# Forming the values of an attention step two visits later, with four transposed-probability tiles

## The chip, the cores and the metric

The kernel runs on one core of one Trainium2 chip. The metric is the device time of one execution in microseconds (us). Before the change it was 578.66 us, the median of 3 runs (578.45 to 579.55). One more execution was recorded by the hardware profiler; all times of single instructions below are from that one.

## What is computed

Attention over 4 batches, 8 heads, 768 positions and head size 64, with a mask that keeps the first 8 positions and the 96 nearest earlier ones, and a bias that falls with the distance. The result, reshaped to 3072 tokens of 512 channels, goes through a gated feed-forward:

```python
scores = scale * (q @ k.T) + bias            # masked: is_global | is_local
a = softmax(scores);  x = (a @ v) as (3072, 512)
h = ((x @ w1) * (x @ w2)) @ w3
out = h @ w_out
```

The kernel multiplies w3 by w_out once at the start (`fold`), so the feed-forward of a block of tokens is three products: x with w1, x with w2, and their product g with w3·w_out. Each factor is held as a rounded high part and a low part (`split`), and each product takes three matmuls: high by high, high by low, low by high.

## The kernel before, in words

The 12 blocks of 256 query positions (4 batches, 3 blocks each) times 4 pairs of heads make 48 units; two units make a *step*, so there are n = 24 steps, two to a block and four to a pair of blocks (512 tokens). A *visit* is what the program does around one step. Its parts, in the order in which TensorE (PE) gets them:

- `visit` (L541): the scores of step s for its first unit (`scores`, tile `s`), one half of the *values* of step s-1 (`values`, tile `v`: probabilities times v), the scores of the second unit, the other half of the values. Between the halves ScalarE (ACT) writes a few elements of the values' tile (L553), so all that stands behind it on ACT waits for the first half.
- `rows` (L412): VectorE (DVE) adds the bias and finds the row maximum (L424), ACT takes exp (L425). `take` (L531) splits the values of step s-1 into the feed-forward's input `xh`, `xl`, and when a block is complete puts its feed-forward on the list `work`.
- `slices(k)` (L512): k *slices* from that list. A slice is half of a product group: 12 matmuls of 256 columns or 6 of 512, or 6 of the output product. They fill PE while DVE, ACT and the DMA engines bring the probabilities of step s into shape.
- `loads` (L519): SyncE's queue (SP) loads the keys and queries (`qr`) and the v rows (`vr`) of step s+1.
- `softmax` (L428) scales the rows. From step SWAP = 4 on they are then transposed without PE: DVE transposes blocks of 32 by 32 (`swap`, L468) into a tile `ph`, one DMA per unit writes it to a buffer `d` in DRAM (L469), and four DMAs per unit read it back with the blocks exchanged (`back`, L474), into the same `ph`. Only then are the probabilities of step s ready for `values` in visit s+1.

The first four steps (`first_steps`, L579) run beside the preparation of the weights (`weights`, `convert`, `fold`) and transpose on PE (`flip`). The order on PE, and on ACT from visit 4 on, is the order in which the program is written; on DVE and SP it is so in the first steps, and later a scheduler places DVE's and SP's instructions. An engine and a queue run what they hold in order: a DMA on SP that waits holds up all DMAs behind it.

Buffers: `ph` has 2 tiles (those of one step), `vr` 4 (two steps), `qr` 2, `a` and `g` of the feed-forward 2 each. The table `SLICES` says how many slices each visit has: 10 in visit 3, 9 in visits 4 to 7, 12 from visit 8 on. The first two blocks give 24 slices each and every later pair of blocks 48, so 12 per visit use up what four visits bring; what the last pair leaves is run at the end.

Of the kernel before, what the change touches and what calls it, by code (L numbers as in the profile page):

```python
# [10 lines left out]
F32 = mybir.dt.float32  # L11
# [9 lines left out]
P = 128  # L21
NP = H // 2
NQ = 2
# [46 lines left out]
class FeedForward:  # L70
# [29 lines left out]
    def weights(self, *names):  # L100


        pieces, fresh = [], []
        for kind, *at in names:
            if kind == "w":
                f, n = divmod(at[0], 2)

                raw = self.stage[{3: 0, 5: 2, 6: 0}[f] + n] if f in (3, 5, 6) else self.raws[:, n]
                dst, src = self.t3s[:, at[0] % 4], self.src[n][f]
                fresh.append((n, f, dst.bitcast(F32).rearrange("p (i m) -> p i m", i=NCC)))  # L110
            elif kind == "o":
                dst, src = self.wo[:, at[0]], self.w_out[at[0]]
            else:
                f, z = at
                dst = self.mp.tile([P, PC], I32, tag=self.next(0, "agagoo"), name=f"t3_{f}_{z}")
                src = self.w3t[f, :, z * PC:(z + 1) * PC]
                self.t3[f, z] = dst
            if kind != "w":
                raw = self.next(1, self.stage + self.first)
            pieces.append((dst, raw, src))  # L120
        convert(self.nc, pieces)
        self.lows()
        for n, f, x in fresh:
            hi, lo = (w[:, f] for w in self.w[n])
            self.nc.scalar.activation(hi, x, AF.Copy)
            self.late.append((lo, x, hi))
        if names[0] == ("o", NFC - 2):

            self.first = []
# [22 lines left out]
    def run(self, c, xh, xl, row, width):  # L152
# [4 lines left out]
        for f0 in range(0, NFC, nf):  # L157
            fs = slice(f0, f0 + nf)
            for n in range(2):
# [9 lines left out]
                if n == 0:  # L169
                    a = mp.tile([P, nf, width], F32, tag="a", name=f"a_{c}_{f0}")  # L170
                    nc.scalar.activation(a, ps, AF.Copy)  # L171
                    yield
            g = mp.tile([P, nf, width], F32, tag="g", name=f"g_{c}_{f0}")
            nc.vector.tensor_tensor(out=g, in0=ps, in1=a, op=ALU.mult)  # L174
            split(nc, gh[:, fs], gl[:, fs], g)
            yield
# [151 lines left out]
def banded(ctx, tc, ff, ns, nt, nf, oki, ident, qk, vx):  # L328
# [6 lines left out]
    ld = ctx.enter_context(tc.tile_pool(name="ld", bufs=STEP))  # L335
    at = ctx.enter_context(tc.tile_pool(name="at", bufs=2))
    ps_s = ctx.enter_context(tc.tile_pool(name="ps_s", bufs=1, space=PSUM))
    ps_v = ctx.enter_context(tc.tile_pool(name="ps_v", bufs=1, space=PSUM))
# [9 lines left out]
    def biases():  # L348
        it = at.tile([P, UW], I32, tag="ph", name="it")
        itg = at.tile([P, P], I32, tag="ph", name="itg")  # L350
        rel, loc = (at.tile([P, UW], F32, tag="pr", name=n) for n in ("rel", "loc"))
# [38 lines left out]
    def load_values(c, hp):  # L390
        b, cb = divmod(c, NCB)
        nw = 2 * NQ if cb else 2 * NQ - 1
        vr = ld.tile([P, 2 * NQ, 2 * D], F32, tag="vr", bufs=2 * STEP, name=f"vr_{c}_{hp}")
        nc.sync.dma_start(out=vr[:, :nw], in_=vx[b, cb, hp, :, :nw])
        return vr
# [59 lines left out]

    def swap(c, hp, pr):

        first = c % NCB == 0  # L460
        x = at.tile([P, 2, NB, NQ * 2, BK], F32, tag="ph", name=f"ph_{c}_{hp}")
        d = dr.tile([NB, BK, 2, NB, NQ * 2 * BK], F32, tag="d", name=f"d_{c}_{hp}")
# [77 lines left out]

    def visit(s, ahead):  # L541


        uu = spread(s - 1) if s else None
        ps = [None, None]
# [4 lines left out]
        def half(k):  # L550
            if s:
                if k:
                    nc.scalar.activation(uu[:, :, T], ident[:, :STEP], AF.Copy)  # L553
                values(uu, s - 1, k)

# [7 lines left out]
        return ps, uu  # L563

    def first_visit(s):
        ps, uu = visit(s, False)
        if s:
            take(s - 1, uu)
        return ps
# [4 lines left out]
    def turn(s, i, prs):  # L574
        c, hp = pairs(s)[i]
        phs.setdefault(s, []).append(at.tile([P, NQ * 2, 2, P], F32, tag="ph", name=f"ph_{c}_{hp}"))
        flip(c, hp, prs[i][0], phs[s][i])

    def first_steps():  # L579
# [27 lines left out]
        ff.weights(("o", 6), ("o", 7))  # L607
        loads(0, keys=False)
        prs = all_rows(0, ps)
# [9 lines left out]
        def scale(s):  # L619
            for p, r in zip(pairs(s), prs):  # L620
                softmax(*p, *r, nc.scalar)
            loads(s + 1)

# [53 lines left out]

    SLICES = [()] * 3 + [(5, 3, 2)] + [9] * 4 + [12] * (n - 8)
    with tc.manual_schedule(engines={mybir.EngineType.PE}):
        with tc.manual_schedule(engines={mybir.EngineType.DVE, mybir.EngineType.SP}):  # L680
            first_steps()
        with tc.manual_schedule(engines={mybir.EngineType.Activation}):
            for s in range(4, n):
                ps, uu = visit(s, True)
                rs = []
                for i, p in enumerate(pairs(s)):
                    rs.append(rows(*p, ps[i]))
                    if i == 0:
                        take(s - 1, uu)
                slices(2)  # L690
                loads(s + 1)
                xd = []
                for p, r in zip(pairs(s), rs):
                    softmax(*p, *r, nc.vector)
                    xd.append(swap(*p, r[0]))
                for x, d in xd:
                    back(x, d)
                phs[s] = [x for x, _ in xd]
                slices(SLICES[s] - 2)
            uu = spread(n - 1)  # L700
            values(uu, n - 1, 2)
            take(n - 1, uu)
            slices(10 ** 6)
# [45 lines left out]
```

## Time and profile before

| | before |
|---|---|
| median of 3 runs | 578.66 us |
| the profiled execution: device time | 575.89 us |
| its span (first to last instruction) | 574.0 us |
| PE busy | 537.0 us (94%) |
| DVE busy | 308.8 us (54%) |
| ACT busy | 243.1 us (42%) |
| moved by DMA | 96.06 MB, mean 167 GB/s |
| PE waiting for `ph<-d` before a values matmul | 13.3 us in 9 waits |

PE is the engine that is nearly always at work; matmuls are pipelined, so its busy share says that it is seldom without work, not that each matmul runs at peak. The program has three stretches: to about 107 us the weights are prepared (DVE is busy 47 to 48 of every 50 us), from 107 to 499 us steps 4 to 23 are visited, and from 499 us to the end there is only feed-forward. The granted clock of TensorE is given as a share of full speed: 1.00 is the upper of its two levels (2.4 GHz), 0.50 the lower (1.2 GHz).

### The profile page before, as it was taken

Reading aid. Unit: us, or ns where it says so; the run is one execution under the profiler, and the core shown is the slowest. Engines: PE = TensorE matmul, PEld = TensorE weight load, DVE = VectorE, ACT = ScalarE, POOL = GpSimd, SP = SyncE. Lnnn points to the kernel's source line nnn. Section 1 sums busy time; section 2 is a strip of 40 time slices with the busy share of each in tenths; the row PEclk is TensorE's granted clock in tenths of the full one; section 3 lists DMA queues with packets and bytes.
Section 4 is the critical chain, followed back from the end, with each engine's and each line's share of the span. In section 5 each row is a group of like instructions: output and inputs, shape, how many; then the busy total and the mean of one; then the engine's idle time right before and its main releaser. Section 6 shows DMA issues by size and latency. Waiting matters only on the chain.

```text
span 574.0 us, 11298 instructions
## 1 busy us (share of the span) xinstructions
PE 537.0 (94%) x4280; PEld 429.1 (75%) x4280; DVE 308.8 (54%) x931; ACT 243.1 (42%) x716; POOL 5.0 (1%) x22
## 2 busy tenths in 40 slices
PE   1999998979888999999999999999999998999995
PEld 0445547968887888888888888888888886888884
DVE  8999999644543574554447624754365565012200
ACT  3065687525442554345435424553355344122210
POOL 0000000000000000000000000000000000000000
PEclk9999999998989999999999999999999999999998
DMA  8897654254466646456554576455665542500011
GB/s 299 302 362 273 226 222 155 84 165 173 142 198 201 199 139 187 158 191 197 174 165 168 163 222 207 139 139 173 212 221 156 169 152 81 176 19 1 1 38 42
DMA packets 72527, 96.06 MB, mean 167 GB/s; under 512 B 5904, under 2 KB 48912, under 8 KB 72464
## 3 DMA queue, kind: packets, MB, share of 16 engines
q1 hardware_dynamic: 72464, 95.25, 50.8%
q8 instruction: 36, 0.59, 0.5%
q14 instruction: 27, 0.22, 0.1%
HBM read 67.96 MB, written 27.26 MB: 166 GB/s over the span
## 4 chain that ended last, share of the span: by engine, by line
PE 58%; DMA 12%; ACT 10%; DVE 9%; SPq 8%; issue 2%; DVEq 0%; ACTq 0%
PE m L164 8%; PE m L165 8%; PE m L166 8%; SPq L474 7%; PE o L181 7%; PE o L182 6%; PE o L183 6%; DMA ph<-d 6%; ACT pr L425 6%; PE w L145 5%; PE v L502 5%; DMA d<-ph 4%; PE s L409 3%; ACT pr L437 1%; DMA stage<-w3t 1%
## 5 line engine op out<-in xcount | busy, mean ns | idle before, releaser
L425 ACT ACTIVATE pr<-pr,mx 128x232 f32<-128x232 f32 (+1 forms) x192 | 88.1, 461 | 23.3 <-DVE mx L424 23.3
L424 DVE CUSTOM_DVE_ANT_0 pr<-s,biasw 128x232 f32<-128x232 f32 x160 | 54.3, 395 | 55.6 <-PE s L409 55.4
L164 PE MATMUL m<-xh,w2h 128*128 128x512 f32 (+1 forms) x224 | 81.6, 364 | 1.4 <-DVE g L174 1.4
L174 DVE TENSOR_TENSOR g<-m,a 128x512 f32<-128x512 f32 x48 | 32.9, 685 | 92.4 <-PE m L166 92.4
L164 PE MATMUL m<-xh,w1h 128*128 128x512 f32 (+1 forms) x224 | 81.2, 363 | 0.3 <-ACT a L171 0.3
L165 PE MATMUL m<-xl,w1h 128*128 128x512 f32 (+1 forms) x224 | 80.6, 360 | 0.0
L166 PE MATMUL m<-xh,w1l 128*128 128x512 f32 (+1 forms) x224 | 80.5, 360 | 0.0
L166 PE MATMUL m<-xh,w2l 128*128 128x512 f32 (+1 forms) x224 | 80.4, 359 | 0.0
L165 PE MATMUL m<-xl,w2h 128*128 128x512 f32 (+1 forms) x224 | 80.4, 359 | 0.0
L66 ACT ACTIVATE gh<-g 128x512 fp32r<-128x512 f32 x48 | 30.3, 632 | 114.0 <-DVE g L174 114.0
L181 PE MATMUL o<-wh,gh 128*128 128x512 f32 x192 | 76.2, 397 | 0.0
L182 PE MATMUL o<-wl,gh 128*128 128x512 f32 x192 | 75.1, 391 | 0.0
L183 PE MATMUL o<-wh,gl 128*128 128x512 f32 x192 | 74.9, 390 | 0.0
L145 PE MATMUL w<-wo,t 128*128 128x512 f32 x128 | 59.5, 619 | 11.7 <-DVE wo L61 11.3
L502 PE MATMUL v<-ph,vr 64*64 64x64 f32 (+4 forms) x1408 | 48.9, 253 | 16.6 <-DMA ph<-d 13.3
L502 PEld LDWEIGHTS v<-ph,vr 64*64 64x64 f32 (+3 forms) x1408 | 44.2, 138 | 21.2 <-DMA ph<-d 7.4
L145 PEld LDWEIGHTS w<-wo,t 128*128 128x128 f32 x128 | 24.5, 197 | 41.5 <-issue 24.9
L67 DVE TENSOR_TENSOR gl<-g,gh 128x512 fp32r<-128x512 f32 x48 | 33.2, 693 | 29.4 <-ACT gh L66 29.4
L468 DVE STREAM_TRANSPOSE ph<-pr 128x512 f32<-128x512 f32 x80 | 46.6, 640 | 3.9 <-ACT pr L437 2.8
L164 PEld LDWEIGHTS m<-xh,w2h 128*128 128x128 f32 x224 | 42.3, 189 | 8.2 <-DVE g L174 1.6
L164 PEld LDWEIGHTS m<-xh,w1h 128*128 128x128 f32 x224 | 42.6, 190 | 7.1 <-ACT a L171 0.5
L171 ACT ACTIVATE a<-m 128x512 f32<-128x512 f32 x48 | 28.4, 592 | 45.0 <-PE m L166 45.0
(86 smaller groups left out, 682.1 us busy)
## 6 DMA issues: line engine op xcount, KB each, us to landing
d<-ph SPq DMA_DIRECT2D x40, 512.0 KB, 2.7
ph<-d SPq DMA_DIRECT2D x160, 128.0 KB, 3.2
qr<-qk SPq DMA_DIRECT2D x32, 312.0 KB, 3.1
vr<-vx SPq DMA_DIRECT2D x32, 256.0 KB, 4.2
stage<-w3t SPq DMA_DIRECT2D x15, 512.0 KB, 6.3
out_dram<-ot SPq DMA_DIRECT2D x24, 256.0 KB, 2.8
raws<-w SPq DMA_DIRECT2D x10, 512.0 KB, 5.7
qr<-qk SPq DMA_DIRECT2D x16, 260.0 KB, 3.3
```

The costliest lines, as they stand in the source:

```text
L145: nc.tensor.matmul(ps, lhsT=self.t3[f, z][:, i * P:(i + 1) * P].bitcast(F32), rhs=self.wo[:, k].bitcast(F32), start=k == 0, stop=k == NFC - 1)
L164: nc.tensor.matmul(ps[:, z], lhsT=mh, rhs=xh[:, i], start=i == 0, stop=False)
L165: nc.tensor.matmul(ps[:, z], lhsT=mh, rhs=xl[:, i], start=False, stop=False)
L166: nc.tensor.matmul(ps[:, z], lhsT=ml, rhs=xh[:, i], start=False, stop=i == NCC - 1)
L181: nc.tensor.matmul(ps, lhsT=gh[:, f, ts], rhs=self.wh[:, f], start=f == 0, stop=False)
L182: nc.tensor.matmul(ps, lhsT=gh[:, f, ts], rhs=self.wl[:, f], start=False, stop=False)
L183: nc.tensor.matmul(ps, lhsT=gl[:, f, ts], rhs=self.wh[:, f], start=False, stop=f == NFC - 1)
L424: nc.vector.tensor_tensor_reduce(out=pr[:, j, u, w0:], in0=ps[u][:, j, w0:UW], in1=bias, scale=-SCALE, scalar=3.0e38, op0=ALU.add, op1=ALU ...
L425: nc.scalar.activation(pr[:, j, u, w0:], pr[:, j, u, w0:], AF.Exp, bias=m, scale=-1.0, accum_out=sm[:, j, u:u + 1])
L468: nc.vector.transpose(x[:, k, :, u0:], units[:, u0:, k0:k0 + P].rearrange("p u (b c) -> p b u c", c=BK))
L474: nc.sync.dma_start(out=x[b * BK:(b + 1) * BK].rearrange("r k a u c -> r k a (u c)"), in_=d[:, :, :, b].rearrange("a r k e -> r k a e"))
L502: nc.tensor.matmul(uu[u * D:(u + 1) * D, i, j * P + q:j * P + q + n], lhsT=v[r], rhs=x[:, q // step:(q + n) // step][r], start=k != 1 and ...
```

## The change

The values of step s are formed in visit s+2 instead of s+1. Steps 0 to 3 keep their old place (the values of step 3 are formed in visit 4); visit 5 therefore forms no values, visit 6 those of step 4, and so on; after visit 23 come the values of step 22, 12 slices, and the values of step 23 (`last_visit`).

So two steps' probabilities live at once: `ph` gets two tags, `ph0` and `ph1`, of two tiles each. The v rows of step s are loaded one visit later than before (with visit s+1), and `vr` has 2 tiles instead of 4. The two `g` tiles go: the product is written over `a`. Two of the early w3 tiles, which used the place of `g`, use that of `ph1`. As a block is complete one visit later, visits 4 to 8 have 7, 7, 7, 7 and 8 slices (36 in all, before 9, 9, 9, 9 in visits 4 to 7) and 12 from visit 9 on.

```diff
-            g = mp.tile([P, nf, width], F32, tag="g", name=f"g_{c}_{f0}")
-            nc.vector.tensor_tensor(out=g, in0=ps, in1=a, op=ALU.mult)
-            split(nc, gh[:, fs], gl[:, fs], g)
+            nc.vector.tensor_tensor(out=a, in0=ps, in1=a, op=ALU.mult)
+            split(nc, gh[:, fs], gl[:, fs], a)
...
-        vr = ld.tile([P, 2 * NQ, 2 * D], F32, tag="vr", bufs=2 * STEP, name=f"vr_{c}_{hp}")
+        vr = ld.tile([P, 2 * NQ, 2 * D], F32, tag="vr", name=f"vr_{c}_{hp}")
...
-    def visit(s, ahead):
+    def visit(s, sv, ahead):
-        uu = spread(s - 1) if s else None
+        uu = None if sv is None else spread(sv)
...
-            if s:
+            if uu is not None:
...
-                values(uu, s - 1, k)
+                values(uu, sv, k)
...
+    def last_visit(s):
+        uu = spread(s)
+        values(uu, s, 2)
+        take(s, uu)
...
-        loads(0, keys=False)
         prs = all_rows(0, ps)
...
-            loads(s + 1)
+            loads(s + 1, vals=False)
+            loads(s, keys=False)
...
-    SLICES = [()] * 3 + [(5, 3, 2)] + [9] * 4 + [12] * (n - 8)
+    SLICES = [()] * 3 + [(5, 3, 2)] + [7, 7, 7, 7, 8] + [12] * (n - 9)
...
-            for s in range(4, n):
-                ps, uu = visit(s, True)
+            for s in range(SWAP, n):
+                sv = s - 1 if s == SWAP else s - 2 if s > SWAP + 1 else None
+                ps, uu = visit(s, sv, True)
...
-                loads(s + 1)
+                loads(s + 1, vals=False)
+                if s > SWAP:
+                    loads(s - 1, keys=False)
...
-                    xd.append(swap(*p, r[0]))
+                    xd.append(swap(*p, r[0], f"ph{s % 2}"))
...
-            uu = spread(n - 1)
-            values(uu, n - 1, 2)
-            take(n - 1, uu)
+            last_visit(n - 2)
+            loads(n - 1, keys=False)
+            slices(SLICES[n - 1])
+            last_visit(n - 1)
             slices(10 ** 6)
```

What this makes of the order on PE is seen in visit 6. The rows stand as the program has them: line, operation, output<-inputs with their numbers, and the columns. Before, behind the scores of the first unit (`s`), come the values of step 5 (`ph_2`, `ph_3` with `vr_2`, `vr_3`):

```order
L409 MATMUL s_101<-qr_0_1340 64x168
L409 MATMUL s_102<-qr_0_1340 64x168
L502 MATMUL v_2_1457<-ph_2_1354,vr_2_1139 64x128 x2
L502 MATMUL v_2_1457<-ph_3_1365,vr_3_1141 64x128 x2
L502 MATMUL v_2_1457<-ph_2_1354,vr_2_1139 64x64 x2
L502 MATMUL v_2_1457<-ph_3_1365,vr_3_1141 64x64 x2
```

After the change, in the same place, they are the values of step 4 (`ph_0_1138` and `ph_1_1149`, written in visit 4):

```order
L410 MATMUL s_101<-qr_0_1274 64x168
L410 MATMUL s_102<-qr_0_1274 64x168
L503 MATMUL v_0_1351<-ph_0_1138,vr_0_1278 64x128 x2
L503 MATMUL v_0_1351<-ph_1_1149,vr_1_1280 64x128 x2
L503 MATMUL v_0_1351<-ph_0_1138,vr_0_1278 64x64 x2
L503 MATMUL v_0_1351<-ph_1_1149,vr_1_1280 64x64 x2
```

Nothing else of the attention moves on PE: scores and values alternate as before, with values one step older.

On SP's queue, the DMAs of step 6 before: out to `d` (L469), back into `ph` (L474), then keys (`qr`) and v rows (`vr`) of step 8, then `d` of step 7:

```order
L469 DMA d_0_1573<-ph_0_1572 128x1024
L469 DMA d_1_1585<-ph_1_1584 128x1024
L474 DMA ph_0_1572<-d_0_1573 32x8x128 x4
L474 DMA ph_1_1584<-d_1_1585 32x8x128 x4
L387 DMA qr_0_1791<-qk 128x624
L387 DMA qr_1_1793<-qk 128x624
L394 DMA vr_0_1795<-vx 128x512
L394 DMA vr_1_1797<-vx 128x512
L469 DMA d_2_1806<-ph_2_1805 128x1024
L469 DMA d_3_1818<-ph_3_1817 128x1024
```

After the change (L470, L475, L388, L395 are the same operations), where the scheduler has placed the first key load of step 8 ahead of the way back of step 6, and the v rows are those of step 6:

```order
L470 DMA d_0_1469<-ph_0_1468 128x1024
L470 DMA d_1_1481<-ph_1_1480 128x1024
L388 DMA qr_0_1664<-qk 128x624
L475 DMA ph_0_1468<-d_0_1469 32x8x128 x4
L475 DMA ph_1_1480<-d_1_1481 32x8x128 x4
L388 DMA qr_1_1666<-qk 128x624
L395 DMA vr_0_1668<-vx 128x384
L395 DMA vr_1_1670<-vx 128x384
L470 DMA d_2_1679<-ph_2_1678 128x1024
L470 DMA d_3_1691<-ph_3_1690 128x1024
```

The key load takes the place of the tile that the first scores of visit 7 read, so the way back of step 6 now stands behind those scores. The v rows of step 6 follow it, and are wanted in visit 8.

## Rows read from the trace of the kernel before

**Rows 1.** The page's head: the span and its instructions, and the busy time of each engine with its share and its instructions.

```profile
span 574.0 us, 11298 instructions
PE 537.0 (94%) x4280; PEld 429.1 (75%) x4280; DVE 308.8 (54%) x931; ACT 243.1 (42%) x716; POOL 5.0 (1%) x22
```

**Rows 2.** Whom PE waited for in the whole program: us in total, number of waits, the longest.

```profile
PE v L502 <- DMA ph<-d: 13.3, 9, 3.6
PE w L145 <- DVE wo L61: 11.3, 1, 11.3
...
PE m L164 <- DVE g L174: 1.4, 1, 1.4
```

**Rows 3.** Busy time by stretches that begin with the first scores of a visit: visits 4 to 8 (9, 9, 9, 9 and 12 slices), and visits 11 and 12. Columns: the stretch in us from the span's start, its length, busy us of PE, weight loads, DVE, ACT and GpSimd with their instructions, the granted clock, the DMA engines' share, GB/s.

```profile
107.15:122.67 15.52, 15.52 (x187) 14.37 (x186) 10.29 (x33) 8.32 (x26) 0.00 (x0) 1.00 0.47 158
122.67:145.42 22.75, 18.52 (x176) 16.44 (x175) 7.62 (x29) 7.76 (x25) 0.00 (x0) 0.85 0.57 175
145.42:163.98 18.56, 16.17 (x206) 15.69 (x205) 9.87 (x34) 8.44 (x27) 0.63 (x2) 1.00 0.55 166
163.98:182.83 18.85, 16.79 (x157) 14.73 (x156) 8.59 (x32) 7.37 (x26) 0.60 (x2) 0.91 0.60 182
182.83:203.69 20.86, 19.39 (x161) 15.99 (x163) 10.47 (x33) 8.92 (x27) 0.00 (x0) 1.00 0.65 195
243.02:262.51 19.49, 19.49 (x173) 16.25 (x175) 7.70 (x29) 7.66 (x25) 0.00 (x0) 1.00 0.63 192
262.51:281.72 19.21, 19.21 (x173) 15.90 (x175) 9.39 (x33) 8.52 (x27) 0.60 (x2) 1.00 0.56 179
```

**Rows 4.** PE's waits in two stretches: visits 4 to 8 (107 to 204 us) and visits 9 to 23 (204 to 500 us).

```profile
PE v L502 <- DMA ph<-d: 10.2, 5, 3.6
...
PE v L502 <- DMA ph<-d: 3.2, 4, 2.3
```

**Rows 5.** Single microseconds behind a wait for `ph<-d`, columns as in rows 3: two in visit 5, one in visit 6, one in visit 7. The granted clock stands ahead of the last two numbers.

```profile
128.00:129.00 1.00, 0.86 (x22) 0.89 (x25) 0.00 (x0) 0.00 (x0) 0.00 (x0) 0.50 0.04 13
132.00:133.00 1.00, 1.00 (x4) 0.83 (x3) 0.93 (x6) 0.76 (x2) 0.00 (x0) 0.50 0.69 223
...
148.00:149.00 1.00, 0.25 (x11) 0.28 (x15) 0.31 (x2) 0.00 (x0) 0.00 (x0) 1.00 0.57 209
...
168.00:169.00 1.00, 1.00 (x31) 1.00 (x28) 0.42 (x3) 1.00 (x6) 0.00 (x0) 0.50 0.00 0
```

**Rows 6.** The chain of waits through visit 4 into visit 5, in order of time (start us, us, what): scores and values of visit 4, the DMA to `d`, the last DMA back, and the values that waited.

```profile
107.15 0.73 PE s L409 x16
107.89 0.71 PE v L502 x31
...
117.32 2.63 DMA d<-ph
120.09 0.69 SPq L474
...
124.82 3.19 DMA ph<-d
128.14 1.33 PE v L502 x18
```

**Rows 7.** SP's queue in the same stretch, in order of time: start, us until the last of the group was issued (with waits), what.

```profile
107.97 1.57 SPq L387 DMA_DIRECT2D qr<-qk  x2
109.84 0.80 SPq L394 DMA_DIRECT2D vr<-vx  x2
117.32 1.51 SPq L469 DMA_DIRECT2D d<-ph  x2
120.09 5.34 SPq L474 DMA_DIRECT2D ph<-d  x8
125.54 5.67 SPq L387 DMA_DIRECT2D qr<-qk  x2
```

**Rows 8.** The page's DMA issues: KB of each, and the median us from issue to landing. The last two are loads of the first 107 us, where many stand in the queues at once.

```profile
qr<-qk SPq DMA_DIRECT2D x32, 312.0 KB, 3.1
vr<-vx SPq DMA_DIRECT2D x32, 256.0 KB, 4.2
stage<-w3t SPq DMA_DIRECT2D x15, 512.0 KB, 6.3
...
stage_xl<-w3t SPq DMA_DIRECT2D x1, 512.0 KB, 10.2
```

**Rows 9.** From the first steps: a pair of v loads in SP's queue (of step 1), and DVE's one wait for a weight load soon after.

```profile
27.94 1.25 SPq L394 DMA_DIRECT2D vr<-vx  x2
...
36.66 0.43 DVE L57 TENSOR_SCALAR t<-stage 128x512 int32<-128x512 int32 x1 [0.31 <-DMA stage<-w3t]
```

**Rows 10.** The feed-forward's groups behind the last visit: ACT's copy into `a` of one group, and of the group two later; between them, from DVE, the subtraction that ends the first group.

```profile
505.22 0.60 ACT L171 ACTIVATE a<-m 128x512 f32<-128x512 f32 x1 [2.07 <-PE m L166]
...
509.40 0.69 DVE L67 TENSOR_TENSOR gl<-g,gh 128x512 fp32r<-128x512 f32 x1 [0.70 <-ACT gh L66]
...
516.16 0.60 ACT L171 ACTIVATE a<-m 128x512 f32<-128x512 f32 x1 [1.35 <-PE m L166]
```

**Rows 11.** From the chain near the end: the second half of the values in visit 23, and the values of step 23, which are formed whole.

```profile
480.38 0.69 PE v L502 x31
...
497.62 1.91 PE v L502 x32
```

More of the change, by code (lines that the diff above doesn't have):

```diff
@@ L114, in weights @@
                 f, z = at
-                dst = self.mp.tile([P, PC], I32, tag=self.next(0, "agagoo"), name=f"t3_{f}_{z}")
+                tag = self.next(0, ("a", "ph1", "a", "ph1", "o", "o"))
+                dst = (self.mp if tag in "ao" else self.at).tile([P, PC], I32, tag=tag, name=f"t3_{f}_{z}")
                 src = self.w3t[f, :, z * PC:(z + 1) * PC]
@@ L336, in banded @@
     at = ctx.enter_context(tc.tile_pool(name="at", bufs=2))
+    ff.at = at
     ps_s = ctx.enter_context(tc.tile_pool(name="ps_s", bufs=1, space=PSUM))
@@ L348, in biases @@
     def biases():
-        it = at.tile([P, UW], I32, tag="ph", name="it")
-        itg = at.tile([P, P], I32, tag="ph", name="itg")
+        it = at.tile([P, UW], I32, tag="ph0", name="it")
+        itg = at.tile([P, P], I32, tag="ph0", name="itg")
         rel, loc = (at.tile([P, UW], F32, tag="pr", name=n) for n in ("rel", "loc"))
@@ L454, in flip, with swap @@
         nc.scalar.activation(ph[:, m0:], pt[:, m0:], AF.Copy)
-    def swap(c, hp, pr):
+    def swap(c, hp, pr, tag):
         first = c % NCB == 0
-        x = at.tile([P, 2, NB, NQ * 2, BK], F32, tag="ph", name=f"ph_{c}_{hp}")
+        x = at.tile([P, 2, NB, NQ * 2, BK], F32, tag=tag, name=f"ph_{c}_{hp}")
         d = dr.tile([NB, BK, 2, NB, NQ * 2 * BK], F32, tag="d", name=f"d_{c}_{hp}")
@@ L563, in visit @@
         return ps, uu
+    def last_visit(s):
+        uu = spread(s)
+        values(uu, s, 2)
+        take(s, uu)
     def first_visit(s):
-        ps, uu = visit(s, False)
+        ps, uu = visit(s, s - 1 if s else None, False)
         if s:
@@ L575, in turn @@
         c, hp = pairs(s)[i]
-        phs.setdefault(s, []).append(at.tile([P, NQ * 2, 2, P], F32, tag="ph", name=f"ph_{c}_{hp}"))
+        phs.setdefault(s, []).append(at.tile([P, NQ * 2, 2, P], F32, tag="ph0", name=f"ph_{c}_{hp}"))
         flip(c, hp, prs[i][0], phs[s][i])
@@ L687, in banded @@
                     rs.append(rows(*p, ps[i]))
-                    if i == 0:
-                        take(s - 1, uu)
+                    if i == 0 and uu is not None:
+                        take(sv, uu)
                 slices(2)
-                loads(s + 1)
+                loads(s + 1, vals=False)
+                if s > SWAP:
+                    loads(s - 1, keys=False)
                 xd = []
```

## The prediction

> **What bounds the kernel now.** I read the page's head first. TensorE (PE) is busy 537.0 of 574.0 us and every other engine below 310 [rows 1], so the time is PE's work plus PE's idle time, and the change adds no work to speak of. Then the list of PE's waits: the longest sum is 13.3 us in 9 waits of a values matmul for `ph<-d`, the probabilities on their way back from DRAM; the next, 11.3 us, is one wait at the start on the weights' preparation [rows 2]. Split by stretch, 10.2 us of the 13.3 lie in visits 4 to 8 and 3.2 us in visits 9 to 23, of which 2.3 us is a single wait [rows 4]. So most visits with 12 slices cover the way to DRAM and back, and those with 9 do not.
>
> The chain shows why. Visit 4 begins its scores at 107.15, the first DMA to `d` starts at 117.32, the eight issues back run from 120.09, the last lands at 124.82 + 3.19 = 128.0, and the values of visit 5 start at 128.14 [rows 6]: 21.0 us from scores to usable probabilities. Visit 5 itself had begun at 122.67, and a visit with 9 slices that waits for nothing takes 15.52 us [rows 3]. SP's queue shows that nothing foreign delays this way: the eight issues take 5.34 us by themselves [rows 7].
>
> A second cost hangs on the same waits. After the wait of visit 5 the granted clock is 0.50, the lower of its two levels (1.2 GHz), for the microseconds in which PE works again (128 to 133 us), and again at 168 us; after the wait of visit 6 it stays 1.00 [rows 5].
>
> **The change, part by part.** The sum is made against the profiled execution, 575.89 us (its span of 574.0 and 1.9 around it). The median, 578.66, is 2.8 us above that; I take the gain off the median.
>
> 1. *Waits and clock in visits 4 to 8.* These five visits last from 107.15 to 203.69, 96.5 us. Their work without hindrance: visit 4 shows 15.5 us for 9 slices, PE busy throughout, and visits 11 and 12 show 19.2 to 19.5, say 19.35, for 12 [rows 3]. 4 x 15.5 + 19.35 = 81.4. The loss is 15.1 us: 10.2 of waits [rows 4], and 4.9 of slower clock and restarts. After the change the same slices and values are run, only 12 slices and one set of values later, so if every visit runs unhindered all 15.1 come back.
>
> Do they? From visit 6 on the probabilities have until the visit after next. A visit with 7 slices takes 15.5 less two slices; a slice is (19.35 - 15.5)/3 = 1.28 us, so 13.0 us, and visit 5, without values (0.71 and 0.69 us for its halves [rows 6, 11]), 11.6 us. Two of them, 24.6 us or more, exceed the 21.0 us from scores to values. `ph<-d` is no longer late.
>
> 2. *Later waits.* The 3.2 us in visits 9 to 23 [rows 4] go the same way: a way that is 2.3 us late has some 19 us more.
>
> 3. *The start.* One pair of v loads falls out of SP's queue ahead of w3 loads (1.25 us of issue for such a pair); DVE's one wait for such a load nearby was 0.31 us [rows 9]. DVE sets the pace there, so I count 0.3 us and not 1.25.
>
> 4. *What is late next: the v rows.* They now have 2 tiles instead of 4 and stand, by SP's order after the change, behind the key load that waits for the first scores of visit s, then the eight returns, then a second key load. In visit 7: 0.73 us for those scores [rows 6], 0.8 for the key load, 5.3 for the returns, 0.8, and 0.8 for the two v issues [rows 7]: 8.4 us into the visit. With a landing of 4.2 us [rows 8] they are there at 12.6, and wanted at 13.0 + 0.7 = 13.7: 1.1 us to spare. In visit 8, with 8 slices, 2.4 us; in visit 6, where the order is the plain one but two key loads and an output go ahead, about as little as in visit 7. Ends: nothing lost (4.2), 2.0 us with the 6.3 us that the weight loads took, and 13.4 us (4.9, 4.9, 3.6) with the longest landing of the page, 10.2 [rows 8]. The DMA engines will be busier: 15.5 to 22.8 us of visit at a share of 0.47 to 0.65 [rows 3] is some 11 us of full work a visit, now in 13. I take 1.0 us, near the 4.2, halfway to the 6.3.
>
> The Trainium skill, in "DMA: Bandwidth & Descriptors", section "Latency and other measured facts", speaks against the lower end: it gives the access to HBM 0.2 us on average and up to 2 us under high load. By it, as an estimate, landings would grow by up to 1.8 us and the loss would be 1.4 us; by the row's 4.2, taken where the share was some 0.6, it is nothing. No run here shows the denser case.
>
> 5. *The end.* The values of step 22 are now also formed whole: 1.91 us instead of 0.71 + 0.69 [rows 6, 11], 0.5 us lost. The v rows of step 23 have 12 slices to arrive.
>
> 6. *At nothing.* The product over `a`: a copy into `a` must now wait for the subtraction two groups earlier. In the tail that ends at 510.1 and the copy comes at 516.16 [rows 10], 6.1 us of cover; at a visit's start up to 4 us of row work may stand between, and each microsecond beyond would be PE's. If the cover were gone, 40 groups at half a microsecond would cost 20 us; the nearest row for PE waiting on such a product is a single 1.4 us [rows 2]. The w3 tiles under another tag keep their number of buffers.
>
> Sum: 15.1 + 3.2 + 0.3 - 1.0 - 0.5 = 17.1 us. 575.89 - 17.1 = 558.8 for a profiled execution; 578.66 - 17.1 = **561.6 us** for the median.
>
> **The rivals.**
>
> *A. The wait changes its name.* PE waits for `vr` instead of `ph` in visits 7 to 9. For it: the 1.1 us to spare, one queue, and a DMA share that rises from some 0.6 to 0.85. Against it: 4.2 us was measured with the same neighbours in the queue. With a landing of 8.2 us, between the two last rows of [rows 8], the visits are 2.9, 2.9 and 1.6 us late, 7.4 in all, and one slower clock more, at (15.1 - 10.2)/2 = 2.5 us for each of the two drops: gain 18.6 less 0.5 less 9.9 = 8.2 us, 570.5 us; with the landing of 10.2 us, 13.4 and 2.5 are lost, and the time is 576.5 us.
>
> [...]
>
> *B. DVE or ACT becomes the bound of the short visits.* DVE is busy 7.6 to 10.5 us a visit, ACT 7.3 to 8.9 [rows 3]; in 13 us that is up to 0.8 and 0.7. PE would then wait for its products' tiles. Against it: DVE's work spreads with the slices, and two fewer bring less of it. Nearest price: the 1.4 us of [rows 2], in each of four visits 5.6 us: gain 11.5, 567.2 us.
>
> *C. Slower than before: SP's queue becomes the ring.* The key load ahead of the returns ties the way back of step s to the scores of visit s+1, and the v rows to those returns. The ring from first scores to first scores is 7.7 us of queue plus the landing. With a landing L the three short visits lose 3 x (7.7 + L - 13.0) and the fifteen visits of 12 slices 15 x (7.7 + L - 19.35) where that is positive. From L = 11.3 the first term alone, 18, eats the gain; at 13 us both are 23 + 20, 43 us, less 18: 604 us. The longest landing seen is 10.2, and that among the loads of the start.
>
> *D. No change.* The waits turn out to sit in visits that the new order only moves. Against it: the order on PE shows the older values in every visit from 6 on. 578.7 us.
>
> **How the numbers follow.** The forecast, 558.5 to 565.5, gets 0.71, A 0.14 (565.5 to 577), B 0.06, C 0.05, D 0.04. Runs of this kernel lie within 0.2% (578.45 to 579.55), so a change below 1.2 us can't be told from none. Faster takes the forecast, A and B: 0.91; same D: 0.04; slower C: 0.05. The upper bound of the gain is 15.1 + 3.2 + 0.3 = 18.6, or 560; 1.5 us for what is unseen gives 558.5 as the low end. The high end at 568.5 takes in B and a third of A and leaves out about 0.18.
>
> **What would show it.** Right: no line PE `v` <- DMA `ph<-d` above 1 us; visits 4 to 8 of 13.0, 11.6, 13.0, 13.0 and 14.2 us, so that visit 9 begins near 172; granted clock 1.00 through 120 to 190 us; PE busy about 96%. Wrong in step 4: PE waits for `vr<-vx`, with `vr` landing above 5 us. Wrong in step 6: PE or ACT waits for `gl`, or an `a` copy that PE waits for. Wrong in step 1: visits of 15 us or more with DVE or ACT as the releaser. The forecast is wrong if the gain is below 13 us, or if it exceeds 20: then work beside the waits has gone that I did not see.

## The result, and the profile after

| | before | after |
|---|---|---|
| median | 579.11 us (4 runs, 578.45 to 581.46) | 554.75 us (4 runs, 554.14 to 556.77) |
| ratio, 95% interval | | 0.9579 [0.9541, 0.9616] |
| profiled execution, its span | 575.89, 574.0 us | 554.55, 552.8 us |

The change makes the kernel faster by 24.4 us. The forecast was 561.6, with 558.5 as the low end: the direction is right, the gain is larger than forecast, and the time lies outside the range. One of the runs of before that were made beside the experiments had a granted clock of 0.66 and took 773.3 us; it is left out everywhere.

The page's head after the change, which answers to [rows 1]:

```profile
span 552.8 us, 11214 instructions
PE 528.0 (96%) x4248; PEld 422.4 (76%) x4248; DVE 308.1 (56%) x931; ACT 243.0 (44%) x715; POOL 4.9 (1%) x22
```

Of the 21.2 us by which the span fell, PE's idle time gave 12.2 (37.0 before, 24.8 now) and its *busy* time 9.0 (537.0 and 528.0). Yet only 32 of 4280 matmuls went (step 22's values, formed whole, take 32 instead of 64). So 9.0 us of what the first profile called busy was loss too. Part of it is the slower clock that the prediction counted (as 4.9 us in visits 4 to 8), part is waiting that the profile shows as busy time, as is seen below.

PE's waits in the whole program, us in total, number, the longest, against [rows 2]:

```profile
PE w L146 <- DVE wo L61: 11.8, 2, 11.2
PE v L503 <- ACT ph L455: 3.1, 3, 1.1
PE m L165 <- DVE a L174: 1.4, 1, 1.4
```

The line on `ph<-d`, 13.3 us in 9 waits before, is gone, and no line on `vr` has come. The wait for the weights at the start stays. The 1.4 us on the product is the same wait as before, now on `a`.

Visits 4 to 8, and visit 11, by stretches with the columns of [rows 3]:

```profile
107.32:120.19 12.87, 12.87 (x175) 12.18 (x174) 9.60 (x32) 8.17 (x26) 0.00 (x0) 1.00 0.44 150
120.19:131.28 11.09, 11.09 (x76) 8.87 (x75) 7.50 (x29) 6.04 (x22) 0.00 (x0) 1.00 0.82 258
131.28:144.16 12.88, 12.88 (x181) 12.59 (x180) 7.90 (x31) 7.88 (x26) 0.63 (x2) 1.00 0.76 229
144.16:156.94 12.78, 12.78 (x181) 12.49 (x180) 9.16 (x33) 7.21 (x25) 0.57 (x2) 1.00 0.88 284
156.94:170.67 13.73, 13.73 (x146) 11.93 (x145) 8.91 (x31) 7.81 (x25) 0.00 (x0) 1.00 0.83 258
209.00:228.24 19.24, 19.24 (x173) 16.02 (x174) 11.56 (x35) 9.56 (x28) 0.00 (x0) 1.00 0.64 184
```

PE is busy in all of each stretch, and the granted clock is 1.00 where [rows 3] had 0.85 and 0.91. The DMA share rises to 0.88. Over the whole program the median landings hardly move; the page's DMA issues, against [rows 8]:

```profile
ph<-d SPq DMA_DIRECT2D x160, 128.0 KB, 3.3
qr<-qk SPq DMA_DIRECT2D x32, 312.0 KB, 3.6
vr<-vx SPq DMA_DIRECT2D x32, 256.0 KB, 3.8
```

In the stretch from 122 to 190 us alone they get longer, the write to `d` most of all. Before the change (the first two rows) and after it:

```profile
ph<-d SPq DMA_DIRECT2D x30, 128.0 KB, 3.2
d<-ph SPq DMA_DIRECT2D x6, 512.0 KB, 2.7
...
d<-ph SPq DMA_DIRECT2D x10, 512.0 KB, 4.7
ph<-d SPq DMA_DIRECT2D x38, 128.0 KB, 3.8
```

**Where the second part of the gain was hidden.** I measured the *attention part* of each visit, from the start of its first score matmul to the start of the first matmul of its slices. Starts are records, ends of matmuls are modelled. Unhindered, scores and values take 2.41 to 2.69 us, by which head blocks they touch.

| attention part, us | before | after |
|---|---|---|
| visits 4 to 8 | 2.66, 9.35, 5.41, 5.56, 4.25 | 2.65, 1.30 (no values), 2.62, 2.52, 2.47 |
| visits 9 to 22, range | 2.40 to 3.53 | 2.41 to 2.69 |
| visit 23 | 5.41 | 2.69 |

The slices behind it take 16.54 to 16.60 us for 12 in both kernels. In visits 9 to 23 the attention parts lost 6.8 us before (4.1 in visits 9 to 22, 2.7 in visit 23), not the 3.2 of [rows 4]. Visit 10 shows why. PE's timeline before (start us, us, matmuls, count, and in brackets the idle time ahead):

```profile
222.86 0.80 PE L409 MATMUL s<-qr 64*64 64x168 f32 x16
223.48 0.39 PE L502 MATMUL v<-ph,vr 64*64 64x128 f32 x4
224.31 0.77 PE L502 MATMUL v<-ph,vr 40*64 40x128 f32 x24 [0.43 <-DMA ph<-d]
```

and the same visit after:

```profile
189.74 0.80 PE L410 MATMUL s<-qr 64*64 64x168 f32 x16
190.36 0.85 PE L503 MATMUL v<-ph,vr 64*64 64x128 f32 x32
```

Without a wait 32 value matmuls follow each other in 0.85 us. Before, four of them fill 0.39 us, because a matmul that nothing follows is shown to its modelled end, and only then do the 0.43 us begin that are called idle. The attention part was 0.88 us longer (3.53 against 2.65). The waits of visits 6 and 8, behind which the clock stayed at 1.00, are understated in the same way: 2.4 and 1.5 us in the list, 2.8 and 1.8 us of attention part lost. The Trainium skill, "Trainium Kernel Development and Optimization", section "Performance Expectations", calls matmul busy time a bad metric for the distance from the roofline, because matmuls are pipelined; here 9.0 of the 21.2 us gained had stood as busy time, the slower clock's part included.

### The profile page after: what moved, and what is told of

Its sections match the earlier page's. It is cut to its first block, busy times and chain, and to the rows that moved or that the text cites. A ratio compares the mean times of both kernels' runs of the same rounds, so it can differ in the third digit from the quotient of the medians.

```text
span 552.8 us, 11214 instructions
## 1 busy us (share of the span) xinstructions
PE 528.0 (96%) x4248; PEld 422.4 (76%) x4248; DVE 308.1 (56%) x931; ACT 243.0 (44%) x715; POOL 4.9 (1%) x22
## 4 chain that ended last, share of the span: by engine, by line
PE 89%; DVE 7%; DMA 2%; ACT 1%; SPq 0%; issue 0%; ACTq 0%; DVEq 0%
PE m L165 16%; PE m L166 15%; PE m L167 15%; PE o L181 8%; PE o L182 8%; PE o L183 8%; PE v L503 6%; PE w L146 6%; PE s L410 5%; DMA stage<-w3t 1%; DVE t L59 1%; DVE t L61 1%; DVE wo L59 1%; DVE wo L61 1%; PE t L449 1%; DMA nt<-ns 1%
## 5 line engine op out<-in xcount | busy, mean ns | idle before, releaser
L174 DVE TENSOR_TENSOR a<-m,a 128x512 f32<-128x512 f32 x48 | 32.9, 686 | 82.5 <-PE m L167 82.3
L66 ACT ACTIVATE gh<-a 128x512 fp32r<-128x512 f32 x48 | 30.3, 632 | 109.3 <-DVE a L174 109.3
L146 PE MATMUL w<-wo,t 128*128 128x512 f32 x128 | 58.5, 609 | 12.3 <-DVE wo L61 11.8
L146 PEld LDWEIGHTS w<-wo,t 128*128 128x128 f32 x128 | 24.1, 194 | 41.7 <-issue 24.8
L67 DVE TENSOR_TENSOR gl<-a,gh 128x512 fp32r<-128x512 f32 x48 | 33.3, 693 | 28.9 <-ACT gh L66 28.9
L469 DVE STREAM_TRANSPOSE ph<-pr 128x512 f32<-128x512 f32 x80 | 46.6, 640 | 3.2 <-ACT pr L438 1.6
L167 PEld LDWEIGHTS m<-xh,w2l 128*128 128x128 f32 x224 | 42.3, 189 | 6.4
L167 PEld LDWEIGHTS m<-xh,w1l 128*128 128x128 f32 x224 | 42.3, 189 | 6.3
```

The lines of the kernel that those rows point to most:

```text
L67: nc.vector.tensor_tensor(out=lo, in0=x, in1=hi.bitcast(F32), op=ALU.subtract)
L146: nc.tensor.matmul(ps, lhsT=self.t3[f, z][:, i * P:(i + 1) * P].bitcast(F32), rhs=self.wo[:, k].bitcast(F32), start=k == 0, stop=k == NFC - 1)
L167: nc.tensor.matmul(ps[:, z], lhsT=ml, rhs=xh[:, i], start=False, stop=i == NCC - 1)
L469: nc.vector.transpose(x[:, k, :, u0:], units[:, u0:, k0:k0 + P].rearrange("p u (b c) -> p b u c", c=BK))
```

## The experiments

Theory 1: the gain is all distance. A step's probabilities need some 21 us, sometimes more, and the values now come later than that everywhere. The rivals, one or two for each run: the product over `a` gives something; the table of slices does it by itself; only visits 4 to 8 count; the clock, not the waits, is the cost; the late visits' excess is an accident of one execution.

**The distance only from visit 9 on (e1_late).** From the changed kernel, with `LATE` = 8; the slices in the table are moved to fit.

```diff
-                sv = s - 1 if s == SWAP else s - 2 if s > SWAP + 1 else None
+                sv = s - 1 if s <= LATE else s - 2 if s > LATE + 1 else None
...
-                if s > SWAP:
-                    loads(s - 1, keys=False)
+                if s != LATE:
+                    loads(s if s < LATE else s - 1, keys=False)
```

> The values come two visits later only from visit 9 on; visits 5 to 8 keep the old order with 9 slices, and visits 8 to 12 share 48 slices (10, 10, 10, 9, 9). Theory 1 (the gain is TensorE's waits for the probabilities and the slower clock behind them, and the part of it that the forecast missed is short waits in the visits with 12 slices, hidden under the modelled ends of matmuls): visits 5 to 8 stay as before (scores and values 9.4, 5.4, 5.6, 4.3 us), those of visits 10 to 23 fall from 2.4 to 3.5 (5.4 in visit 23) to 2.4 to 2.7; span shorter by 6.8 - 0.6 = 6.2 us, median 573 us. Rival 2 (the missed part comes from the v rows being loaded later, or from the product over a, anywhere in the program): those parts stay near 2.9 on average and the span falls by no more than 3 us.

Measured: 573.39 us, ratio 0.9916 [0.9882, 0.9949], span 570.8. Visits 5 to 8 lose as before (attention parts 8.89, 7.28, 5.11, 3.91) and visits 10 to 23 lie at 2.41 to 2.69 again. All waits for `ph<-d` that are left stand between 107 and 204 us; PE's waits in that stretch:

```profile
PE v L504 <- DMA ph<-d: 9.3, 4, 3.5
PE v L504 <- DVE mx L426: 0.6, 1, 0.6
```

So the late visits give what was said of them. The span gains only 3.2 us, since this order starts visit 4 some 1.5 us later, waits 1 us in visit 9 and forms step 22's values whole.

**The distance only up to visit 9 (e2_early).** From the changed kernel, with `BACK` = 9; in visit 9 the values of steps 7 and 8 are both formed, and from visit 10 on those of the step before.

```diff
-                sv = s - 1 if s == SWAP else s - 2 if s > SWAP + 1 else None
+                sv = s - 1 if s == SWAP or s > BACK else s - 2 if s > SWAP + 1 else None
...
-                    loads(s - 1, keys=False)
+                    loads(s if s > BACK else s - 1, keys=False)
...
-                slices(SLICES[s] - 2)
-            last_visit(n - 2)
-            loads(n - 1, keys=False)
-            slices(SLICES[n - 1])
+                if s == BACK:
+                    slices(7)
+                    last_visit(s - 1)
+                    loads(s, keys=False)
+                    slices(3)
+                else:
+                    slices(SLICES[s] - 2)
```

> The values come two visits later only in visits 6 to 9, with the 7, 7, 7, 7, 8 slices; the values of step 8 are formed whole near the end of visit 9, and from visit 10 on all is as before the change. Theory 1: visits 4 to 8 take 63 to 65 us as in the changed kernel, the scores and values of visits 10 to 23 last 2.4 to 3.5 us and 5.4 in visit 23 again; span 574.0 - 15.3 + 0.5 = 559.2 us, median 561 to 563. Together with the kernel that has only the late part it makes up the whole gain. Rival 2: the late visits stay short here too, and the span comes near 555.

Measured: 569.45 us, ratio 0.9882 [0.9833, 0.9931], span 567.2: 8 us above what was expected. Visits 4 to 8 are those of the changed kernel (63.3 us in all). The excess is in the late visits: visit 10, where the order changes over, has 6.55 us of attention, and visits 16 and 19 have 5.62 and 6.30. PE's waits from 107 us on:

```profile
PE v L504 <- DMA ph<-d: 6.4, 5, 2.5
PE v L504 <- DVE mx L426: 1.8, 1, 1.8
```

and the chain ahead of visit 19's wait:

```profile
363.82 4.75 DMA d<-ph
```

The write to `d` lasts 4.75 us here, where [rows 6] had 2.63. The same is seen before the change ahead of the 2.3 us wait in visit 23; the chain there:

```profile
466.12 4.56 DMA d<-ph
470.69 0.56 SPq L474
```

A way of 21.0 us plus 2 us of slow write overshoots a visit of 19.2 plus 0.7; that of step 22 took 22.8 us before the change. The changed kernel has more such writes: 15 of its 40 take over 4 us from issue to landing, before 3 of 40. SP waits up to 4.2 us for one (before 3.0), the longest way, that of step 9, takes 29.3 us from scores to the last landing, and no PE wait follows. Without the distance the late visits lose 13.6 us in this execution, 3.9 of it at the changeover, so 9.7 against the 6.8 before: I had expected one execution's 6.8 to be the rule.

**Only the product over `a` (e3_over_a).** From the kernel before:

```diff
-            nc.vector.tensor_tensor(out=g, in0=ps, in1=a, op=ALU.mult)
-            split(nc, gh[:, fs], gl[:, fs], g)
+            nc.vector.tensor_tensor(out=a, in0=ps, in1=a, op=ALU.mult)
+            split(nc, gh[:, fs], gl[:, fs], a)
```

> The kernel before with one edit: the product is written over a, and g is not used. Theory 1: no change, ratio 1.000 within 0.002, and no wait of ScalarE or TensorE on the subtraction. Rival 2 (the product over a gives part of the gain): 2 to 4 us faster. The rival of the prediction that it costs: slower by more than 1 us.

Measured: 578.23 us, ratio 0.9996 [0.9969, 1.0024]. This edit neither gives nor costs anything; it only makes room.

**The kernel before once more (e8_before_again).**

> The kernel before, unchanged, for a second trace. Theory 1 (the late visits are at the edge, so that a single late write to the DRAM buffer costs there, and this differs between executions): visits 4 to 8 together within 1.5 us of 96.5, the rest of the difference from 574.0 in scores and values of visits 9 to 23 above 2.7 us, each with a write to d that took over 4 us behind it, or in the granted clock. Rival 5 (the spread between executions is spread evenly, over slices too): slices of the 12-slice visits differ from 16.55 us.

Measured, in a single run: 576.88 us, span 575.1. Visits 4 to 8 last 96.71 us together (96.54 in the first profile), visits 9 to 22 have 2.40 to 3.48, visit 23 has 5.26. The slices behind them last 16.54 to 16.59 us. The excess is no accident of one execution. Slow writes to `d` explain little of it, and, against what was expected, they come at the same places again: in both executions those over 4 us are of steps 12 and 22, and only visit 23 waits behind one. In the first profile the probabilities of steps 9 to 21 land 19.1 to 20.8 us behind their scores, on either side of the 19.9 us (19.2 plus 0.7) at which they are wanted.

**Only the table of slices undone (e5_old_slices).** From the changed kernel:

```diff
-    SLICES = [()] * 3 + [(5, 3, 2)] + [7, 7, 7, 7, 8] + [12] * (n - 9)
+    SLICES = [()] * 3 + [(5, 3, 2)] + [9] * 4 + [12] * (n - 8)
```

> The changed kernel with the old table of slices (9, 9, 9, 9, then 12): visit 8 then finds only 2 slices, since the next block is complete in visit 9. Theory 1 (TensorE bounds the changed kernel only as long as each visit has slices enough to cover the ring over the SP queue, some 12 us): visits 4 to 7 last 15.6, 13.9, 15.5, 15.5 us without waits; in visit 8 (5.3 us of TensorE's work) or at the start of visit 9 TensorE waits 4 to 7 us for v rows or probabilities, perhaps with one drop of the clock; span 552.8 + 4 to 9, 557 to 562 us. Rival 4 (the table is not needed, the later values do it alone): span 552 to 554.

Measured: 566.4 us, ratio 0.9782 [0.9726, 0.9837], span 564.6: 11.8 us of the 21.2 are lost, more than the 4 to 9 expected. Only two slices are left for visit 8, which lasts 9.98 us; visit 9 takes 22.62. The waits there:

```profile
PE s L410 <- DMA qr<-qk: 4.4, 1, 4.4
PE v L503 <- DMA vr<-vx: 1.3, 1, 1.3
```

Behind them the granted clock falls (0.87 over visit 9). Later no two slices are left when a pair of blocks becomes complete, and PE waits there for `xl` (up to 0.7 us). So the later values need the new table: a block complete one visit later must leave slices for the visit in between.

**Visits too short for the queue (e6_short).** The same line of the changed kernel:

```diff
-    SLICES = [()] * 3 + [(5, 3, 2)] + [7, 7, 7, 7, 8] + [12] * (n - 9)
+    SLICES = [()] * 3 + [(5, 3, 2)] + [4, 4, 4, 4, 20] + [12] * (n - 9)
```

> The changed kernel with 4 slices in each of visits 4 to 7 and 20 in visit 8. TensorE's work in those visits is 8.2 us (6.9 in visit 5). Theory 1: the ring of 7.7 us of queue and the landing of the v rows, 3.8 to 4.2 us, holds visits 6 and 7 at 11.5 to 12.5 us; TensorE waits 3 to 4 us in visits 6 to 8 each, released by vr or ph DMAs; span 552.8 + 6 to 12, 559 to 565 us. It shows how far the 12.8 us of the visits with 7 slices are from the edge. Rival A of the prediction (the v rows land later than 6 us in the denser stretch): more than 15 us slower.

Measured: 573.32 us, ratio 0.9899 [0.9868, 0.993], span 572.7: 19.9 us lost, where 6 to 12 were expected. Visits 4 to 8 last 8.60, 8.76, 15.36, 11.51 and 38.86 us:

```profile
PE v L503 <- DMA vr<-vx: 5.6, 2, 5.4
PE v L503 <- DMA ph<-d: 3.7, 1, 3.7
...
PE v L503 <- issue: 2.5, 2, 2.3
```

Here the rival of the prediction that was slower than before is seen at work, with longer terms than it had. SP's ring of 7.7 us plus a landing (median 4.0 for these v rows) gives 11.7, and visit 7 lasts 11.51, but that is chance. The v rows for visit 7, loaded in visit 6, land at 143.22 and 143.87, up to 3.6 us behind its start (the list has the 2.3 us until the first under `issue`), and its own work takes the rest. The v rows for visit 8 land at 157.93 and 158.44, some 18 us behind the first scores of visit 7: SP waited until 145.17 for a write to `d`, and the v rows took 5.6 us to land. My 6 to 12 us had neither. Visit 6 waits for the probabilities, since visits 4 and 5 together (17.4 us) are shorter than the way of 21.0, and the granted clock averages 0.91 from 151.82 to 190 us, behind the 5.4 us in visit 8.

**Small matmuls in the waits (e4_filler, e7_filler2).** The kernel before, with matmuls of 48 columns into unused columns of a scores' tile: in e4_filler 30 in visit 5 and 15 in visits 6 to 8, issued with the first half of the values.

```diff
+            if m == 4 and k == 0:
+                for _ in range({5: 30}.get(s + 1, 15) if 5 <= s + 1 <= 8 else 0):
+                    nc.tensor.matmul(sc[1][0][:, :, UW:], lhsT=ff.wh[:, 0, :P], rhs=ff.wh[:, 0, :2 * (256 - UW)].rearrange("p (j c) -> p j c", j=NQ), start=True, stop=True)
```

> The kernel before, with extra matmuls of 48 columns (30 in visit 5, 15 in each of visits 6 to 8) behind the fourth values matmul, where TensorE waits for the probabilities; they write columns that nothing reads. Theory 1 (the clock behind the waits costs 4.9 us in the profiled execution, and some 3 us more in the median): the waits stay (visits 5 to 8 begin as late), but the granted clock stays 1.00 from 120 to 190 us; span shorter by 3 to 5 us, median by 5 to 8. Rival 3 (the restart costs as much whatever the clock, or matmuls as small as these do not hold the clock): span within 1 us of 574.0.

Measured: 598.78 us, ratio 1.0357 [1.033, 1.0383]. The edit was misplaced: in visit 5 the fillers start at 129.49, behind the wait and not in it, and delay what follows; the granted clock averages 0.83 from 120 to 190 us, where 1.00 was expected. PE's timeline:

```profile
129.49 6.59 PE L499 MATMUL s<-wh 128*128 128x48 f32 x30
```

In e7_filler2 they stand ahead of the wait, 16 and 8 of them:

```diff
+            if m == 2 and k == 0:
+                for _ in range({5: 16}.get(s + 1, 8) if 5 <= s + 1 <= 8 else 0):
```

> The kernel before with matmuls of 48 columns, this time ahead of the wait: behind the second values matmul of the program, 16 in visit 5 and 8 in each of visits 6 to 8; they write columns that nothing reads. Theory 1: TensorE's idle stretch in visits 5 to 8 gets shorter by 1 to 2 us each while the probabilities land as late as before, the granted clock falls in fewer places, and the span is 2 to 5 us shorter than that of the kernel before. Rival 3 (the clock falls all the same): span within 1.5 us of 574 to 576, or longer.

Measured: 579.66 us, ratio 1.0028 [0.9997, 1.0059]. The idle waits fall:

```profile
PE v L505 <- DMA ph<-d: 8.2, 9, 2.4
```

but the clock falls all the same, now in visits 5, 6 and 7. The mean granted clock in three stretches of 5 us behind the waits:

```profile
125.00:130.00 5.00, 3.55 (x54) 3.45 (x56) 0.09 (x2) 0.23 (x2) 0.00 (x0) 0.63 0.54 148
...
150.00:155.00 5.00, 5.00 (x87) 4.88 (x79) 2.77 (x13) 3.68 (x17) 0.72 (x2) 0.66 0.37 81
...
170.00:175.00 5.00, 5.00 (x65) 4.80 (x55) 3.36 (x17) 4.75 (x20) 0.60 (x2) 0.66 0.59 156
```

So filling part of the wait with small work did not hold the clock; up to 2.4 us of wait were left, and what filling all of it would do is not shown. How much of the 15 us of visits 4 to 8 is clock and how much wait is not measured apart.

**The distance without more tiles (e9_behind, e11_behind2).** The kernel before, with the halves of the values moved behind the first and the second slice of the same visit:

```diff
+                uu = spread(s - 1)
+                ps = [scores(*p, x) for p, x in zip(pairs(s), qrs[s])]
+                rs = [rows(*p, x) for p, x in zip(pairs(s), ps)]
+                slices(1)
+                values(uu, s - 1, 0)
+                slices(1)
+                nc.scalar.activation(uu[:, :, T], ident[:, :STEP], AF.Copy)
+                values(uu, s - 1, 1)
+                take(s - 1, uu)
```

> The kernel before, with one thing moved: the values of step s-1 stay in visit s, but their halves come behind the first and the second slice instead of between the scores (and take behind them); tiles, loads and the table of slices are those of before. Theory 1 (what counts is only the distance from a step's scores to its values, 21.0 us of way against the length of a visit; the short waits of the late visits are of the same kind): the values are wanted some 2.3 us later in every visit, so that visit 5 waits some 2.4 us instead of 4.7, visits 6 to 8 under 1 us each instead of 3.0, 3.2 and 1.8, and the late visits lose under 2 us instead of 6.8. Gain of the span 10 to 16 us, span 558 to 564, ratio to before 0.972 to 0.983. Rival (the gain needs two steps' tiles; values moved back delay the release of the probabilities' two tiles, so that the transposing of step s starts later and the way back ends as much later): waits of ph<-d as long as before, gain under 4 us, ratio above 0.993.

Measured: 616.82 us, ratio 1.0619 [1.0551, 1.0687], slower by far, which neither theory expected. The waits:

```profile
PE v L502 <- ACT v L690: 26.5, 19, 2.3
...
PE v L502 <- DMA ph<-d: 0.6, 1, 0.6
```

The wait for the probabilities is gone (13.3 to 0.6), but ACT's short write into the values' tile (L553 before, L690 here) came too late. ACT's timeline in one such visit:

```profile
302.36 0.63 ACT L66 ACTIVATE gh<-g 128x512 fp32r<-128x512 f32 x1 [1.62 <-DVE g L174]
302.90 0.16 ACT L690 ACTIVATE v<-ident 128x2 f32<-128x2 f32 x1
```

It is behind the first slice's own copy, which waits for DVE. A wait of 0.4 to 2.3 us in 19 visits brings the mean clock from 107 to 500 us down to 0.97, hence a loss larger than the waits. In e11_behind2 the write goes ahead of the second unit's rows:

```diff
+                rs = [rows(*pairs(s)[0], ps[0])]
+                slices(1)
+                values(uu, s - 1, 0)
+                nc.scalar.activation(uu[:, :, T], ident[:, :STEP], AF.Copy)
+                rs.append(rows(*pairs(s)[1], ps[1]))
+                slices(1)
+                values(uu, s - 1, 1)
+                take(s - 1, uu)
```

> As e9_behind (the kernel before, the halves of the values of step s-1 behind the first and the second slice of visit s), but ScalarE's short write into the values' tile is put ahead of the exps of the visit's second unit; in e9_behind it stood behind all exps, and TensorE waited for it in 19 visits (26.5 us, up to 2.3 each). Theory 1 (only the distance from scores to values counts; two steps' tiles are one way to get it): no wait for ph<-d above 1 us but in visit 5, none for ScalarE's write above 0.5 us; each visit pays some 0.3 us for taking up the slices once more (6 us in all), of the 21.9 us lost in visits 4 to 23 some 16 come back: span 562 to 567, ratio to before 0.978 to 0.988. Rival (breaking the slices up brings a new wait wherever the write stands, so that the second set of tiles is the only way here): waits for ScalarE or VectorE of 0.5 us or more in most visits, span above 574.

Measured: 575.08 us, ratio 0.9939 [0.9918, 0.996], span 572.0. (My reason that the write had stood behind the exps was wrong, as the timeline above shows, but moving it cured the wait.) PE's waits from 107 to 500 us are now a single line, all of it in visits 5 and 6:

```profile
PE v L502 <- DMA ph<-d: 2.8, 2, 1.8
```

Visits 4 to 8 gain 8.0 us (88.57 instead of 96.54). But most visits of 12 slices last 19.98 us and not 19.24: PE takes up the slices three times instead of once, 1.60 us for a single slice instead of 1.38 and 0.83 for half the values instead of 0.7. I had put that at 0.3 us a visit; it is 0.74, and eats most of the gain. So the distance removes all but 2.8 us of the waits without a second set of tiles, as Theory 1 says, though the visits, 0.74 us longer, help it by giving the way more time; two steps' tiles buy it without breaking up the slices.

**The changed kernel once more (e10_after_again).**

> The changed kernel once more, to see a second execution of it in the profile. Theory 1 (the slow writes to the DRAM buffer, 4.5 us and more instead of 2.6, come at visits that differ from one execution to the next, and the changed kernel covers them): span within 1 us of 552.8, the attention part of visits 9 to 23 between 2.4 and 2.7 us each and no wait for ph<-d over 1 us, though some write of d again lasts 3.5 us or more. Rival (the first profile was a lucky one): one or two late visits with a wait of 1 to 3 us, span 554 to 557.

Measured: 555.53 us, ratio 0.958 [0.9519, 0.9641], span 553.7. The attention parts of visits 9 to 23 are 2.41 to 2.69 again, with an SP wait of 3.9 us for a write to `d`. Against what was expected, the slow writes don't move about: in both executions of the changed kernel the same 15 take over 4 us (of steps 6 to 10, 12, 13 and 19). What slows them is not shown. One thing is new, in visit 7, PE's timeline:

```profile
144.39 0.73 PE L410 MATMUL s<-qr 64*64 64x64 f32 x16
145.18 0.43 PE L503 MATMUL v<-ph,vr 64*64 64x128 f32 x4
145.80 0.77 PE L503 MATMUL v<-ph,vr 40*64 40x128 f32 x24 [0.18 <-DMA vr<-vx]
```

The v rows are late: listed as 0.18 us, but the attention part is 3.41 instead of 2.52, 0.9 us, as much as this span is longer.

No version here beats the changed kernel. More v tiles beside the four of the probabilities were not tried.

## Why the prediction was wrong in size

By its steps, against the profiled execution (forecast 17.1 us, measured 21.2 of span):

- *Step 1, visits 4 to 8*: right in its sum. 96.54 us before; after, 63.35 us with 12 slices (16.56 us) and one set of values (2.65 - 1.30 = 1.35) less; with them 81.26, so 15.3 came back, forecast 15.1. The visits last 12.87, 11.09, 12.88, 12.78 and 13.73 us, where 13.0, 11.6, 13.0, 13.0 and 14.2 were named. The split into 10.2 us of waits and 4.9 us of clock and restarts was off: visits 6 and 8 kept the clock at 1.00 and still lost more than the list has for them (4.6 against 3.9 us), so some of the 4.9 us was waiting. The section "HAM oscillation — how this bites in real kernels" in the Trainium skill's "TensorE: Matmul & The Clock Gate" has the clock stay up where the matmul work far exceeds the DMA wait; the trace agrees, with 1.00 in every visit.
- *Step 2, later waits*: the term that failed. I took 3.2 us from the list of waits; 6.8 were there and all came back (e1_late, e8_before_again). The list counts from modelled ends, and short waits stand in it as busy time. With the 3.2 us fell the upper bound of 18.6 us, which was made from them. The prediction's own sign of this, a gain above 20 us because work beside the waits has gone, came: what had gone was waiting that is shown as work.
- *Step 3, the start*: forecast a gain of 0.3; visit 4 begins 0.24 us later (107.32, was 107.08).
- *Step 4, late v rows*: the place is right, the 1.0 us was not spent in the first profile, and 0.9 in the second. My margin of 1.1 us was not there for visit 6's load: its v issues end at 140.88, the last lands at 144.45, and values in visit 7 begin at 144.62, 0.2 us later. The v rows of visits 6 to 8 land in 3.8 to 4.2 us, at a DMA share of up to 0.88; in the second execution one took 4.9 us, in e6_short two took 5.6. Before the change those of visits 5 to 8 took 2.5 to 4.6 us. The estimate from the Trainium skill's "DMA: Bandwidth & Descriptors", section "Latency and other measured facts", up to 1.8 us more than 4.2 under load, is an upper limit that all of these stay below.
- *Step 5, the end*: 0.56 us lost, forecast 0.5. *Step 6*: nothing, as e3_over_a shows.
- *The median*: I took the profiled execution's gain off the median. That was the second failure: with 21.2 us, all terms right, it would have said 557.5. The profiled execution of before lay near the low end of its runs (575.89; 52 runs of it beside these experiments reach from 575.8 to 582.5), that of after lies in the middle (554.55 in 554.14 to 556.77). In the runs of before the mean granted clock is 0.982 to 0.990, in those of after 0.995 to 0.999. This fits waits that vary and take the clock with them, and that the change removes; no profile of a long run of before was had, so it stays an inference.

The sum with measured terms: 15.3 + 6.8 - 0.2 - 0.6 - 0.1 (the tail) = 21.2, and some 3 us more between the medians.

Rival A stood closer than the median tells (step 4, e10_after_again), and C shows only with far shorter visits (e6_short). B did not come: DVE and ACT stay at 9.6 us or less in each of visits 4 to 8, and no PE wait there names them. D is out.

## What to carry to other kernels

Measure what a wait costs from the start of a known block to the start of the next, and compare it with the block unhindered; the list of waits is a lower bound where matmuls are pipelined. When a step's data take a way through DRAM, give it the longest way seen as margin, not the usual one, and expect the way to get longer in denser visits; and look whether the margin can be had by distance between whole blocks, since breaking PE's work up costs by itself. Set a forecast of a median on the spread of the runs as well as on one profile.

## What the runs showed of the hardware

- The 512 KB write to the DRAM buffer takes 2.6 us and more from issue to landing: before the change 2.7 us as a median, with 3 of 40 over 4 us (up to 5.2), after it 3.1 us, with 15 of 40 over 4 us (up to 7.2). In two executions of either kernel the slow ones are those of the same steps.
- The granted clock fell behind many waits, but not behind each: in e6_short's visit 7, with 2.3 us listed, and in e11_behind2's visits 5 and 6 (2.8 us together) it stayed 1.00. In e9_behind eight of the nine waits of 1.7 to 2.3 us for ACT were followed by a fall, and none of the ten of up to 0.8 us. Small matmuls ahead of the wait did not keep it up (e7_filler2).
- At the lower clock a filler of 48 columns took 0.22 us (e4_filler, 6.59 us for 30); PE was busy in all of that time, and the granted clock was 0.50 throughout.
